# Decode attention: VectorE scores 12 of 32 columns with one multiply and one sum per chunk, values become the stationary operand, and w1 and w2 share the key and value slots

## The chip, the core and the metric

The kernel runs on one core of a Trainium2 chip. The core has engines that run side by side, each through its own instructions in order: TensorE (PE in the profile; PEld is its loading of stationary operands), VectorE (DVE), ScalarE (ACT), GpSimd (POOL) and SyncE (SP), which here only issues DMA transfers. Sixteen DMA engines move data between HBM and the on-chip memory SBUF; TensorE writes its results into PSUM. The metric is device time in microseconds (us); lower is better.

## What is computed

One token is decoded through an attention block over a key and value cache and a small dense block. Cut to what matters:

```python
# x: (1,1,640); k_cache, v_cache: (1,32,32768,192); wq: (640,6144); wo: (6144,640); all bf16
q = layernorm(x) @ wq                                   # 32 heads of 192
scores = einsum("bhqd,bhkd->bhqk", q, k_cache) * 192**-0.5
o = einsum("bhqk,bhkd->bhqd", softmax(scores), v_cache)
h = x + o.reshape(1, 1, 6144) @ wo
out = h + maximum(layernorm(h) @ w1, 0) @ w2            # w1: (640,1536), w2: (1536,640)
```

The caches hold 805 MB of the 825 MB that the core reads, and each of their elements is used once.

## The kernel before, in words

A head's 32,768 keys are cut into 8 chunks (NC) of 4,096 keys, so there are 256 chunks (G), counted by `g`. In a chunk each of the 128 partitions holds J = 32 whole rows ("columns" below) of 192 elements: 12,288 bytes a partition, 1,536 KB for the keys (`kt`, line 97) and as much for the values (`vt`, line 99). Each of the two has 5 buffers. SP issues all transfers in program order, one queue for everything, and holds back the load of a buffer until the work on its former content is done. Every transfer is spread evenly over the 16 DMA engines: of a `kt` each engine moves 8 rows of 12,288 bytes.

The program is emitted under a hand-written order (`manual_schedule`), one chunk after the other, and each engine follows it:

- `transposes(g)`: the last JP = 10 columns are turned on TensorE, 15 blocks of 128x128, into PSUM (`tp`, line 195), and ScalarE copies them in two pieces to SBUF (`kT`, line 196).
- `pv(g - 1)`: the former chunk's values are multiplied by its probabilities. The probabilities of one column are the stationary operand (128x1), the 192 values of the column the moving one; 32 matmuls add up in one PSUM row `o_ps` (line 245).
- `scores_pe(g)`: with `kT` as the stationary operand and the query (`qm`) as the moving one, 15 matmuls give the scores of the 10 columns (lines 205 to 209); ScalarE takes exp into `pB` and sums it (line 212).
- `scores_dve(g)`: VectorE scores the other 22 columns, one instruction a column that multiplies `kt` by the query spread over partitions (`qb`) and sums along the row (line 225; the profile shows a second instruction for each, DVE_READ_ACCUMULATOR). `exp_dve` takes exp of them into `pA` (line 232).

Once a head the sums of exp (`dsums`) are added over partitions by a matmul (`den_mm`, line 252), VectorE makes the reciprocal (`den_rec`, lines 258 and 259), called in the middle of the next chunk's scores, and ScalarE scales the head's row (`o_scale`, line 265). For every two heads `o_turn` (line 273) turns the row into a column with three transposes and `project` (line 283) multiplies it by `wo`. `q_rows` and `q_spread` prepare the next head's query. w1 and w2 are loaded whole into buffers of their own in the middle of the run (lines 299 and 301). After the last chunk come the last `pv`, `den_mm`, `den_rec`, `o_scale`, `o_turn`, `project`, the second layernorm (lines 130 to 145), the residual put into two PSUM rows (line 336), the first dense layer (line 341), the second one with `h1T` as the stationary operand and rows of w2 moving (lines 346 and 348), the copies to `y_row` and the store (line 353).

Of the kernel before, what the change touches and what calls it, by code (L numbers as in the profile page):

```python
# [13 lines left out]
def kernel(  # L14
# [26 lines left out]
    J = 32  # L41
    CH = P * J
    NC = Sk // CH
    G = H * NC
    JP = 10
    JD = J - JP
    NB = JP * Dh // P
    QG = 4
    assert Sk % CH == 0 and 2 * Dh == 3 * P and JP % 2 == 0 and H % QG == 0 and H % 2 == 0
# [7 lines left out]
    tsb = ctx.enter_context(tc.tile_pool(name="tsb", bufs=3))  # L57
# [36 lines left out]
    def load_kv(g):  # L94
        h, c = divmod(g, NC)
        kt = kpool.tile([P, J * Dh], bf16, name="kt")
        nc.sync.dma_start(out=kt[:], in_=k_hd[h, c * CH:(c + 1) * CH, :].rearrange("(p j) d -> p (j d)", p=P))
        vt = vpool.tile([P, J * Dh], bf16, name="vt")
        nc.sync.dma_start(out=vt[:], in_=v_hd[h, c * CH:(c + 1) * CH, :].rearrange("(p j) d -> p (j d)", p=P))
        kt_t[g], vt_t[g] = kt, vt  # L100

# [9 lines left out]
    ones_col = const.tile([P, 1], f32)  # L111
    nc.vector.memset(ones_col[:], 1.0)
# [7 lines left out]
    dsums = const.tile([P, H, 2 * NC], f32)  # L120
    w1_sb = const.tile([P, DT, Dff], bf16)
    w2_sb = const.tile([P, FT, D], bf16)
    o_pair = [const.tile([1, 2 * Dh], f32, name=f"o_pair{i}") for i in range(2)]
# [25 lines left out]
    with tc.manual_schedule():  # L149
# [37 lines left out]
        def transposes(g):  # L187
            kt = kt_t[g]
            kT = tsb.tile([P, NB, P], bf16, name="kT")
            for b0 in range(0, NB, 8):  # L190
                nb = min(8, NB - b0)
                tp = tps.tile([P, 8, P], bf16, name="tp")
                for b in range(nb):
                    off = JD * Dh + (b0 + b) * P
                    nc.tensor.transpose(out=tp[:, b, :], in_=kt[:, off:off + P], identity=ident_b[:])  # L195
# [3 lines left out]
        def scores_pe(g):  # L199
            kT = kT_t.pop(g)  # L200
            h, c = divmod(g, NC)
            qm = qm_t[h]
            sp = sps.tile([P, JP], f32, name="sp")
# [7 lines left out]
            pB = pcp.tile([P, JP], bf16, name="pB")  # L211
            nc.scalar.activation(out=pB[:], in_=sp[:], func=F.Exp, scale=SCALE,  # L212
# [3 lines left out]
        def scores_dve(g, mid=None):  # L216
            kt = kt_t.pop(g)
            h, c = divmod(g, NC)
            qb = qb_t[h]
            sc = scp.tile([P, JD], f32, name="sc")  # L220
            for j in range(JD):
                if j == 4 and mid is not None:
                    mid()
                st = scp.tile([P, Dh], bf16, name="st")
                nc.vector.scalar_tensor_tensor(out=st[:], in0=kt[:, j * Dh:(j + 1) * Dh], scalar=1.0, in1=qb[:],  # L225
                                               op0=A.mult, op1=A.mult, accum_out=sc[:, j:j + 1])
            return sc

        def exp_dve(g, sc):
            h, c = divmod(g, NC)  # L230
            pA = pcp.tile([P, JD], bf16, name="pA")
            nc.scalar.activation(out=pA[:], in_=sc[:], func=F.Exp, scale=SCALE,  # L232
# [3 lines left out]
        def pv(g):  # L236
            h, c = divmod(g, NC)
# [4 lines left out]
            for jj in range(J):  # L242
                j = jj + JD if jj < JP else jj - JP
                p = pA[:, j:j + 1] if j < JD else pB[:, j - JD:j - JD + 1]
                nc.tensor.matmul(o[:], lhsT=p, rhs=vt[:, j * Dh:(j + 1) * Dh],  # L245
                                 start=(c == 0 and jj == 0), stop=(c == NC - 1 and jj == J - 1))
# [3 lines left out]
        def den_mm(h):  # L250
            d = mm_bank([1, 2 * NC], f32, "den")
            nc.tensor.matmul(d[:], lhsT=ones_col[:], rhs=dsums[:, h, :], start=True, stop=True)  # L252
            den_t[h] = d
# [130 lines left out]
```

## Time and profile before

| | |
|---|---|
| time, median of 3 runs | 2063.01 us (2062.05 to 2064.38) |
| the profiled execution | 2062.24 us |
| its span, first to last instruction | 2060.4 us |
| granted TensorE clock, mean | 0.835 of full speed |
| busy: DVE / PE / PEld / ACT | 78% / 68% / 58% / 32% of the span |
| median from the issue of a `kt` transfer to its landing | 30.5 us |

The busy shares are means over the whole span. DMA share and GB/s by slice tell how fast the cache comes in. A row of a group gives the line, engine, operation, tiles and shapes, the count, then busy time, the mean duration of one in ns and the idle time of the engine before it. A row of the chain of waits gives start, length and what ran. In the timeline "x15" are fifteen instructions merged in one row.

### The profile page before, as it was taken

How to read it: one execution, taken by the hardware profiler on the slowest of the kernel's cores; microseconds unless marked ns; L12 is line 12 of the kernel's file. 1: busy time of each engine (PE TensorE's matmuls, PEld its weight loads, DVE VectorE, ACT ScalarE, POOL GpSimd, SP SyncE). 2: the span in 40 equal slices, each digit the busy share in tenths (PEclk: the TensorE clock that was granted, in tenths of full speed). 3: DMA queues.
4: the chain of work that ended last, by engine and by line, in shares of the span. 5: the costliest groups of instructions: out<-in, count | busy, mean ns of one | idle time of the engine just before them, and what ended most of it. 6: DMA issues, size and time to landing. Idle time of an engine off the chain costs nothing. (4 is left out here: it accounts for less than half of the span.)

```text
span 2060.4 us, 48468 instructions
## 1 busy us (share of the span) xinstructions
PE 1405.5 (68%) x16643; PEld 1193.5 (58%) x16643; DVE 1603.1 (78%) x11352; ACT 651.6 (32%) x1719; POOL 0.7 (0%) x6
## 2 busy tenths in 40 slices
PE   5766666766667666666665666766677667677767
PEld 4555555655555555555555555555566556566555
DVE  6877887778787788777777778887778877788775
ACT  3333333333333233322322333332333323333332
POOL 0000000000000000000000000000000000000000
PEclk9888887788898788888888888898788987878787
DMA  9999999999999999989998999999999989999991
GB/s 395 423 421 420 423 421 423 407 422 420 423 422 357 423 418 423 416 346 425 382 420 344 418 423 421 423 423 393 425 421 422 414 350 423 420 423 417 397 412 77
DMA packets 87844, 828.10 MB, mean 402 GB/s; under 512 B 8619, under 2 KB 21420, under 8 KB 22060
## 3 DMA queue, kind: packets, MB, share of 16 engines
q1 hardware_dynamic: 87596, 825.00, 96.5%
q8 instruction: 130, 2.13, 0.4%
q14 instruction: 118, 0.97, 0.1%
HBM read 824.97 MB, written 0.00 MB: 400 GB/s over the span
## 5 line engine op out<-in xcount | busy, mean ns | idle before, releaser
L225 DVE SCALAR_TENSOR_TENSOR st<-kt,qb 128x192 bf16<-128x192 bf16 x5632 | 1589.7, 350 | 306.7 <-DMA kt<-in_A_k_cache_dram 294.7
L195 PE MATMUL tp<-ident_b,kt 128*128 128x128 bf16 x3840 | 335.3, 255 | 596.6 <-DMA kt<-in_A_k_cache_dram 596.6
L195 PEld LDWEIGHTS <-kt 128*128 128x128 bf16 x3840 | 280.5, 116 | 623.8 <-DMA kt<-in_A_k_cache_dram 623.8
L245 PE MATMUL o_ps<-vt,pA 128*1 128x192 bf16 x5632 | 606.0, 272 | 45.8 <-ACT pA L232 45.6
L245 PEld LDWEIGHTS <-pA 128*1 128x1 bf16 x5632 | 524.9, 95 | 106.4 <-ACT pA L232 55.9
L196 ACT COPY kT<-tp 128x1024 bf16<-128x1024 bf16 (+1 forms) x512 | 465.1, 960 | 347.6 <-PE tp L195 347.3
L225 DVE DVE_READ_ACCUMULATOR st<-kt,qb 128x1 f32 x5632 | 442.4, 79 | 0.1
L245 PE MATMUL o_ps<-vt,pB 128*1 128x192 bf16 x2560 | 354.6, 305 | 0.4 <-ACT pB L212 0.4
L245 PEld LDWEIGHTS <-pB 128*1 128x1 bf16 x2560 | 237.2, 101 | 73.2 <-issue 22.8
L212 ACT ACTIVATE pB<-sp 128x10 bf16<-128x10 f32 x256 | 46.3, 181 | 630.9 <-PE sp L209 627.3
L232 ACT ACTIVATE pA<-sc 128x22 bf16<-128x22 f32 x256 | 56.6, 221 | 397.0 <-DVE st L225 396.8
L205 PEld LDWEIGHTS <-kT 128*128 128x128 bf16 x1280 | 100.0, 96 | 44.2 <-issue 43.3
L205 PE MATMUL sp<-qm,kT 128*128 128x2 bf16 x1280 | 122.3, 166 | 0.4 <-ACT kT L196 0.4
L209 PE MATMUL sp<-qm,kT 128*128 128x1 bf16 x1280 | 118.8, 163 | 0.4 <-ACT kT L196 0.4
L207 PE MATMUL sp<-qm,kT 128*128 128x1 bf16 x1280 | 118.7, 163 | 0.0
L258 DVE TENSOR_REDUCE rec<-den 1x1 f32<-1x16 f32 x32 | 5.2, 162 | 132.8 <-PE den L252 132.8
L207 PEld LDWEIGHTS <-kT 128*128 128x128 bf16 x1280 | 102.6, 96 | 0.0
L209 PEld LDWEIGHTS <-kT 128*128 128x128 bf16 x1280 | 101.4, 95 | 0.5 <-ACT kT L196 0.5
L212 ACT ACTIVATION_READ_ACCUMULATOR pB<-sp 128x1 f32 x256 | 49.9, 195 | 0.1
L232 ACT ACTIVATION_READ_ACCUMULATOR pA<-sc 128x1 f32 x256 | 48.1, 188 | 0.1
L163 PE MATMUL qps<-wq,xn_ln 128*1 128x192 bf16 x160 | 18.7, 248 | 3.3 <-DMA wq<-in_A_wq_dram 3.3
L265 ACT ACTIVATE o_pair<-o_ps,rec 1x192 f32<-1x192 f32 x32 | 13.2, 413 | 8.3 <-DVE rec L259 8.3
(62 smaller groups left out, 145.8 us busy)
## 6 DMA issues: line engine op xcount, KB each, us to landing
kt<-in_A_k_cache_dram SPq DMA_DIRECT2D x256, 1536.0 KB, 30.5
vt<-in_A_v_cache_dram SPq DMA_DIRECT2D x256, 1536.0 KB, 29.0
wq<-in_A_wq_dram SPq DMA_DIRECT2D x8, 960.0 KB, 27.1
wo<-in_A_wo_dram SPq DMA_DIRECT2D x16, 480.0 KB, 28.2
w_sb<-in_B_w_dram SPq DMA_DIRECT2D x2, 1920.0 KB, 32.2
x_row<-in_A_x_dram SPq DMA_DIRECT2D x1, 1.2 KB
out_dram<-y_row SPq DMA_DIRECT2D x1, 1.2 KB
```

What stands on the lines that cost most here:

```text
L163: nc.tensor.matmul(qps[:], lhsT=xnT[:, c:c + 1], rhs=wq[:, c, hh * Dh:(hh + 1) * Dh], start=(c == 0), stop=(c == DT - 1))
L195: nc.tensor.transpose(out=tp[:, b, :], in_=kt[:, off:off + P], identity=ident_b[:])
L196: nc.scalar.copy(out=kT[:, b0:b0 + nb, :], in_=tp[:, 0:nb, :])
L205: nc.tensor.matmul(sp[:, 2 * i:2 * i + 2], lhsT=kT[:, 3 * i + 1, :], rhs=qm[:, 1:3], start=True, stop=False, skip_group_check=True)
L207: nc.tensor.matmul(sp[:, 2 * i:2 * i + 1], lhsT=kT[:, 3 * i, :], rhs=qm[:, 0:1], start=False, stop=False, skip_group_check=True)
L209: nc.tensor.matmul(sp[:, 2 * i + 1:2 * i + 2], lhsT=kT[:, 3 * i + 2, :], rhs=qm[:, 3:4], start=False, stop=True, skip_group_check=True)
L212: nc.scalar.activation(out=pB[:], in_=sp[:], func=F.Exp, scale=SCALE, accum_out=dsums[:, h, 2 * c + 1:2 * c + 2])
L225: nc.vector.scalar_tensor_tensor(out=st[:], in0=kt[:, j * Dh:(j + 1) * Dh], scalar=1.0, in1=qb[:], op0=A.mult, op1=A.mult, accum_out=sc[:, ...
L232: nc.scalar.activation(out=pA[:], in_=sc[:], func=F.Exp, scale=SCALE, accum_out=dsums[:, h, 2 * c:2 * c + 1])
L245: nc.tensor.matmul(o[:], lhsT=p, rhs=vt[:, j * Dh:(j + 1) * Dh], start=(c == 0 and jj == 0), stop=(c == NC - 1 and jj == J - 1))
L258: nc.vector.reduce_sum(out=s[:, 0:1], in_=d[:], axis=mybir.AxisListType.X)
L265: nc.scalar.activation(out=o_pair[(h // 2) % 2][0:1, (h % 2) * Dh:(h % 2 + 1) * Dh], in_=o[:], func=F.Copy, scale=s[0:1, 1:2])
```

## The change

- The last chunk of the last head is split into three chunks of 16, 8 and 8 columns, so that there are 258 chunks. A table `chunks` gives each its head, place, columns (`jc`) and columns for TensorE (`jp`).
- TensorE takes 20 of 32 columns (10 of 16, 4 of 8): 30 transposes, four copies on ScalarE and 30 score matmuls a chunk. VectorE takes 12: one multiply of all 12 columns at once by the query (broadcast) into an f32 tile `pr`, and one sum along the rows.
- `pv` takes the values as the stationary operand, 128x128, and one or two columns of probabilities as the moving one: 48 matmuls a chunk that add up in four PSUM columns `o_ps` [128, 4]. The output is then already a column, in pieces: `o_scale` moves to VectorE and scales them by a reciprocal that is now made on all partitions (`den_mm` with a full f32 matrix of ones), and `o_turn` puts the pieces in place with 10 f32 matmuls by selection matrices (`sel`) that are made at the start.
- `den_rec` and `o_scale` are called after `scores_dve` of the next head's first chunk, not in it. At the end `den_mm` and `den_rec` stand ahead of the last `pv`.
- w1 and w2 have no buffers of their own: they are loaded in four pieces into `kt` and `vt` buffers ahead of the last three chunks. `kT` has two buffers for three.
- The second dense layer has w2 as the stationary operand and gives a column; the residual is added on VectorE, and one transpose makes the rows that are stored.

```diff
+    chunks = []
+    for h in range(H):
+        parts = [(J, 20)] * NC
+        if h == H - 1:
+            parts = [(J, 20)] * (NC - 1) + [(16, 10), (8, 4), (8, 4)]
...
-    tsb = ctx.enter_context(tc.tile_pool(name="tsb", bufs=3))
+    tsb = ctx.enter_context(tc.tile_pool(name="tsb", bufs=2))
+    prp = ctx.enter_context(tc.tile_pool(name="prp", bufs=1))
...
+    def load_w(name, src, pool, tag, c0, c1):
+        t = pool.tile([P, J * Dh], bf16, tag=tag, name=tag)
+        n = src.shape[1]
+        v = t[:, 0:(c1 - c0) * n].rearrange("p (c n) -> p c n", n=n)
+        nc.sync.dma_start(out=v, in_=src.rearrange("(c p) n -> p c n", p=P)[:, c0:c1, :])
...
-            for j in range(JD):
-                if j == 4 and mid is not None:
-                    mid()
-                st = scp.tile([P, Dh], bf16, name="st")
-                nc.vector.scalar_tensor_tensor(out=st[:], in0=kt[:, j * Dh:(j + 1) * Dh], scalar=1.0, in1=qb[:],
-                                               op0=A.mult, op1=A.mult, accum_out=sc[:, j:j + 1])
+            pr = prp.tile([P, JDM, Dh], f32, name="pr")
+            nc.vector.tensor_tensor(out=pr[:, 0:JD, :], in0=kt[:, 0:JD * Dh].rearrange("p (j d) -> p j d", d=Dh),
+                                    in1=qb[:].unsqueeze(1).to_broadcast([P, JD, Dh]), op=A.mult)
+            sc = scp.tile([P, J], f32, name="sc")
+            nc.vector.reduce_sum(out=sc[:, 0:JD], in_=pr[:, 0:JD, :], axis=mybir.AxisListType.X)
...
-                o_t[h] = ops.tile([1, Dh], f32, name="o_ps")
+                o_t[h] = ops.tile([P, 4], f32, name="o_ps")
...
-                nc.tensor.matmul(o[:], lhsT=p, rhs=vt[:, j * Dh:(j + 1) * Dh],
-                                 start=(c == 0 and jj == 0), stop=(c == NC - 1 and jj == J - 1))
+                v = vt[:, j * Dh:(j + 2) * Dh]
+                nc.tensor.matmul(o[:, 0:1], lhsT=v[:, 0:P], rhs=p[:, 0:1],
+                                 start=first, stop=False, skip_group_check=True)
+                nc.tensor.matmul(o[:, 1:3], lhsT=v[:, P:2 * P], rhs=p,
+                                 start=False, stop=False, skip_group_check=True)
+                nc.tensor.matmul(o[:, 3:4], lhsT=v[:, 2 * P:3 * P], rhs=p[:, 1:2],
+                                 start=False, stop=last, skip_group_check=True)
...
-            nc.tensor.matmul(d[:], lhsT=ones_col[:], rhs=dsums[:, h, :], start=True, stop=True)
+            nc.tensor.matmul(d[:], lhsT=ones_mat[:], rhs=dsums[:, h, :], start=True, stop=True)
...
-            nc.scalar.activation(out=o_pair[(h // 2) % 2][0:1, (h % 2) * Dh:(h % 2 + 1) * Dh], in_=o[:],
-                                 func=F.Copy, scale=s[0:1, 1:2])
+            nc.vector.tensor_scalar_mul(out=o_part[h % 4][:], in0=o_t.pop(h)[:], scalar1=s[:, 1:2])
...
-                nc.tensor.transpose(out=ps[:, b:b + 1], in_=o_pair[pr % 2][0:1, b * P:(b + 1) * P],
-                                    identity=ident_f[0:1, 0:1])
+            parts = [(0, "all", e, 0), (0, "u_l", e, 2), (0, "l_u", e, 3),
+                     (1, "l_l", e, 1), (1, "u_l", e, 3), (1, "l_u", o, 0), (1, "u_u", o, 2),
+                     (2, "all", o, 3), (2, "u_l", o, 0), (2, "l_u", o, 1)]
+            for i, (b, w, src, r) in enumerate(parts):
+                nc.tensor.matmul(ps[:, b:b + 1], lhsT=sel[w][:], rhs=src[:, r:r + 1], start=(i == 0), stop=(i == len(parts) - 1),
+                                 skip_group_check=True)
...
+            if g == G - 3:
+                half = (DT + 1) // 2
+                load_w("w1", B_w1, kpool, "kt", 0, half)
+                load_w("w1", B_w1, vpool, "vt", half, DT)
+                load_w("w2", B_w2, kpool, "kt", 0, FT // 2)
+                load_w("w2", B_w2, vpool, "vt", FT // 2, FT)
...
-        pv(G - 1)
         den_mm(H - 1)
         den_rec(H - 1)
+        pv(G - 1)
         o_scale(H - 1)
...
-            nc.tensor.matmul(y_a[:], lhsT=h1T[:, f:f + 1], rhs=w2_sb[:, f, 0:512],
-                             start=False, stop=(f == FT - 1), skip_group_check=True)
-            nc.tensor.matmul(y_b[:], lhsT=h1T[:, f:f + 1], rhs=w2_sb[:, f, 512:D],
-                             start=False, stop=(f == FT - 1), skip_group_check=True)
...
+        for n in range(DT):
+            for f in range(FT):
+                nc.tensor.matmul(yps[:, n:n + 1], lhsT=w_t["w2", f][:, n * P:(n + 1) * P], rhs=h1T[:, f:f + 1],
+                                 start=(f == 0), stop=(f == FT - 1))
```

How instructions stand in the programs is shown at three places. The first is VectorE at the first change of head; rows of the program before (`st` is the product that nobody reads, `sc` the scores, `x180` one row for equal instructions that follow each other):

```order
L145 TENSOR_SCALAR xn_ln_149<-x_col,mv,rs 128x5
L225 SCALAR_TENSOR_TENSOR st,sc<-kt,qb 128x192 x180
L258 TENSOR_REDUCE rec<-den 1x1
L259 RECIPROCAL rec<-rec 1x1
L225 SCALAR_TENSOR_TENSOR st,sc<-kt,qb 128x192 x176
```

The same place in the changed program:

```order
L257 TENSOR_TENSOR pr<-kt,qb 128x2304
L260 TENSOR_REDUCE sc<-pr 128x12
L303 TENSOR_REDUCE rec<-den 128x1
L304 RECIPROCAL rec<-rec 128x1
L309 TENSOR_SCALAR o_part_140<-o_ps,rec 128x4
L257 TENSOR_TENSOR pr<-kt,qb 128x2304
L260 TENSOR_REDUCE sc<-pr 128x12
```

Twenty-two instructions a chunk become two; the reciprocal has moved behind the whole chunk's scores and brings the scaling along, which reads `o_ps`.

The second is TensorE inside `pv`; first the program before, two columns of a chunk (a weight load and a matmul each):

```order
L245 LDWEIGHTS pB
L245 MATMUL o_ps<-vt,pB 1x192
L245 LDWEIGHTS pB
L245 MATMUL o_ps<-vt,pB 1x192
L245 LDWEIGHTS pB
```

and two columns in the changed program:

```order
L286 LDWEIGHTS vt
L286 MATMUL o_ps<-pB,vt 128x1
L288 LDWEIGHTS vt
L288 MATMUL o_ps<-pB,vt 128x2
L290 LDWEIGHTS vt
L290 MATMUL o_ps<-pB,vt 128x1
```

Two pairs of instructions for two columns have become three, with loads of 128x128 values. In all, TensorE has 33,088 instructions in the program before and 56,843 in the changed one; VectorE, which has one row per instruction there, has 646 in the changed one.

The third is SP's queue at the end; the program before, from the last two chunks on:

```order
L97 DMA kt<-in_A_k_cache_dram 128x6144
L99 DMA vt<-in_A_v_cache_dram 128x6144
L97 DMA kt<-in_A_k_cache_dram 128x6144
L99 DMA vt<-in_A_v_cache_dram 128x6144
L353 DMA out_dram<-y_row 1x640
```

and the changed one, from the last whole chunk on:

```order
L113 DMA vt<-in_A_v_cache_dram 128x6144
L123 DMA kt<-in_B_w_dram 128x3x1536
L123 DMA vt<-in_B_w_dram 128x2x1536
L123 DMA kt<-in_B_w_dram 128x6x640
L123 DMA vt<-in_B_w_dram 128x6x640
L110 DMA kt<-in_A_k_cache_dram 128x3072
L113 DMA vt<-in_A_v_cache_dram 128x3072
L110 DMA kt<-in_A_k_cache_dram 128x1536
L113 DMA vt<-in_A_v_cache_dram 128x1536
L110 DMA kt<-in_A_k_cache_dram 128x1536
L113 DMA vt<-in_A_v_cache_dram 128x1536
L399 DMA out_dram<-y_row 5x128
```

The four weight pieces have moved from the middle of the run to a place ahead of the last three, smaller chunks.

More of the change, by code (lines that the diff above doesn't have):

```diff
@@ L331 @@
         hnT = layernorm_col(h_col, "ln2")
-        y_a = ops.tile([1, 512], f32, tag="o_ps", name="y_a")
-        y_b = ops.tile([1, P], f32, tag="o_ps", name="y_b")
-        for c in range(DT):
-            y = y_a[0:1, c * P:(c + 1) * P] if c < 4 else y_b[0:1, :]
-            nc.tensor.matmul(y, lhsT=h_col[:, c:c + 1], rhs=ident_f[:], start=(c == 0 or c == 4),
-                             stop=False, skip_group_check=True)
-        h1ps = mm_bank([P, FT], f32, "h1ps")
+        h1ps = ops.tile([P, FT], f32, tag="o_ps", name="h1ps")
         for f in range(FT):
             for c in range(DT):
-                nc.tensor.matmul(h1ps[:, f:f + 1], lhsT=w1_sb[:, c, f * P:(f + 1) * P], rhs=hnT[:, c:c + 1],
+                nc.tensor.matmul(h1ps[:, f:f + 1], lhsT=w_t["w1", c][:, f * P:(f + 1) * P], rhs=hnT[:, c:c + 1],
                                  start=(c == 0), stop=(c == DT - 1))
```

122 lines of the change are left out of this document (71 added, 51 removed).

## The prediction

> **What bounds the kernel now.** I read the page's totals first, then the stream of transfers by slice and by queue.
>
> ```profile
> span 2060.4 us, 48468 instructions
> PE 1405.5 (68%) x16643; PEld 1193.5 (58%) x16643; DVE 1603.1 (78%) x11352; ACT 651.6 (32%) x1719; POOL 0.7 (0%) x6
> ...
> GB/s 395 423 421 420 423 421 423 407 422 420 423 422 357 423 418 423 416 346 425 382 420 344 418 423 421 423 423 393 425 421 422 414 350 423 420 423 417 397 412 77
> DMA packets 87844, 828.10 MB, mean 402 GB/s; under 512 B 8619, under 2 KB 21420, under 8 KB 22060
> ...
> q1 hardware_dynamic: 87596, 825.00, 96.5%
> q8 instruction: 130, 2.13, 0.4%
> q14 instruction: 118, 0.97, 0.1%
> ```
>
> No engine is full: VectorE works 1603.1 us of 256 chunks, 6.3 us a chunk where a chunk has 2060.4 / 256 = 8.05 us. The transfers look full at 96.5%. Yet the stream runs at 423 GB/s in most slices and at 340 to 400 in a few. At 423 GB/s the 825.00 MB of data take 1950 us. They take far longer, and the end of the stream shows why. The next view sums engines over stretches; its last columns are the share of the 16 DMA engines and GB/s.
>
> ```profile
> core 0: us, PE busy (x) PEld busy (x) DVE busy (x) ACT busy (x) POOL busy (x), PEclk, DMA share, GB/s
> 100.00:300.00 200.00, 137.32 (x1634) 116.93 (x1632) 157.32 (x1117) 63.16 (x167) 0.00 (x0) 0.84 1.01 421
> ...
> 2000.00:2016.00 16.00, 11.59 (x127) 9.62 (x125) 15.09 (x109) 5.87 (x14) 0.00 (x0) 0.79 1.00 423
> ...
> 2028.00:2038.00 10.00, 8.45 (x89) 6.89 (x90) 8.83 (x63) 4.23 (x8) 0.00 (x0) 0.74 0.06 26
> ```
>
> Until 2016 us all engines run. From 2028 to 2038 the share is 0.06, one in sixteen, at 26 GB/s, a sixteenth of 423: **one DMA engine is some 20 us behind the other fifteen** and finishes alone. Every transfer needs all sixteen, so chunks arrive at that engine's pace; the others run ahead until SP may issue no more, and then stop, which makes the slow slices.
>
> What holds it back? The chain of waits gives the last `kt`; its row and those of the tail behind it:
>
> ```profile
> 2005.22 30.06 DMA kt<-in_A_k_cache_dram
> ...
> 2045.35 0.29 PE oT_ps L273 x2
> ...
> 2045.88 0.53 PE attT L283 x15
> 2046.43 0.17 DVE h_col L330
> 2046.62 0.16 DVE st L130
> ...
> 2047.01 0.56 PE ln_ps L134 x2
> 2047.57 1.79 PE y_a L336 x8
> 2049.36 0.43 PE y_b L336 x2
> 2049.79 1.70 PE h1ps L341 x60
> ...
> 2051.75 0.59 PE y_a L346
> ...
> 2057.56 0.58 ACT y_row L351
> ```
>
> The last `kt` lands at 2035.3 us. The `vt` behind it moves 8 x 12,288 bytes an engine, 3.7 us at 26 GB/s: the late engine ends at 2039. It starts at about 2, so it works 2037 us for what takes 1950: 87 us lost. Now the instruction queues. Of PE's 33,286 instructions (matmuls and loads) q8 fetches 130 blocks: 16 KB or 256 instructions a block, 64 bytes each. Blocks of q14 are 0.97 MB / 118 = 8 KB, or 128 instructions; DVE's 11,352 make 88.7 of the 118. **87 us over 88.7 blocks is 0.98 us a block.** The landing records under these views agree: from 90 to 300 us the last landing of a transfer follows the one before by 3.70 us, by 4.67 where a q14 block of VectorE's rhythm (one in 23 us) lies between, and PE's blocks in q8 never delay it. So VectorE's instruction blocks all ride on one DMA engine, which sets the end.
>
> [...]
>
> **The change part by part.** *VectorE's blocks.* 646 instructions for 11,352: 5 blocks for 89. The late engine loses 5 us, not 87, and is late no more: 2039 - 87 = 1952 for an engine that carries none.
>
> *TensorE's blocks.* 56,843 instructions for 33,088: 130 x 56,843 / 33,088 = 223 blocks. One costs 0.4% x 16 x 2060.4 / 130 = 1.0 us of an engine by the q8 row. The packet records add a delay of the packet behind it: an engine that carries one lands 1.53 us late. All on one engine they would cost 130 x 1.0 us, more than the 87 that the latest one lost, so they are spread; in the landings up to 340 us they come round over eight engines in turn (20 blocks: four engines with two, four with three). What is late next is thus each of these eight: 223 / 8 x 1.53 = 42.6 us. Bounds: 14 us if they cost their bytes alone over sixteen engines, 85 over four. I take 42.6, the spread that the landings show: **the stream ends at 1952 + 42.6 = 1994.6.** ScalarE's blocks ride on another engine; its 1,719 instructions become some 2,270, 18 blocks, and remain below that.
>
> *Does the work in a chunk keep up?* A chunk may now take 1995 / 256 = 7.8 us. Durations:
>
> ```profile
> L225 DVE SCALAR_TENSOR_TENSOR st<-kt,qb 128x192 bf16<-128x192 bf16 x5632 | 1589.7, 350 | 306.7 <-DMA kt<-in_A_k_cache_dram 294.7 <-ACT pB L212 5.8 <-ACT pA L232 4.6
> L131 DVE SCALAR_TENSOR_TENSOR sq<-h_col 128x5 f32<-128x5 f32 x1 | 0.2, 156 | 0.0
> L196 ACT COPY kT<-tp 128x1024 bf16<-128x1024 bf16 x256 | 258.2, 1009 | 347.6 <-PE tp L195 347.3
> L196 ACT COPY kT<-tp 128x896 bf16<-128x896 bf16 x256 | 233.2, 911 | 0.0
> L232 ACT ACTIVATE pA<-sc 128x22 bf16<-128x22 f32 x256 | 56.6, 221 | 397.0 <-DVE st L225 396.8
> 1007.94 1.78 PE L195 MATMUL tp<-ident_b,kt 128*128 128x128 bf16 x15 [3.96 <-DMA kt<-in_A_k_cache_dram]
> 2040.61 0.18 PE L205 MATMUL sp<-qm,kT 128*128 128x2 bf16 x1
> 2040.97 0.16 PE L209 MATMUL sp<-qm,kT 128*128 128x1 bf16 x1
> ```
>
> VectorE: 192 elements take 350 ns and 5 take 156, so 1.04 ns an element and 0.15 us beside. The multiply and the sum pass 2304 elements each: 0.15 + 2.39 = 2.54 us, 5.1 together. No row shows either at this size; from below the bound is half the slope each (2.7 us, if paired 16-bit elements went through at once), from above twice (9.9 us, if f32 counted double). I take 5.1, the row's slope. ScalarE: three copies of 1.009 and one of 768 elements, 0.81 by the two copy rows, are 3.8 us; two exp of some 0.4 with their accumulator reads make 4.6. TensorE: fifteen transposes take 1.78 us at the low clock, thirty 3.6. Fifteen score matmuls of one or two columns start within 0.36 us, 26 ns apart; 48 in `pv` take 1.25 us and 30 for scores 0.8: 5.6 in all, where `pv` alone took 2.8 or more. In a row, eight transposes (0.9), the copies (3.8) and the scores (0.8) make 5.5 to 6 us from chunk to chunk. All are under 7.8, so they lie under the stream. `kt` comes free after 2.5 us of VectorE instead of 6, so SP's queue is served no later. The added waits: `den_rec` waits on VectorE for `den_mm` behind PE's scores, some 0.7 us once a head, with the next chunk's multiply behind it; `o_turn`, 10 f32 matmuls, some 4.5 us of PE for every two heads. The 1.8 us of slack a chunk hide both within three chunks; without it they would cost 16 x 5 = 80 us. Weights in `kt` and `vt` buffers: the last `vt` waits for the `pv` of the last whole chunk, which waits for the 16-column `kt`; by the bytes between, it is issued some 2 us before its turn. I cost this at nothing, 2 us at most.
>
> *The tail.* Before, 2060.4 - 2039 = 21.4 us after the stream. Now the last `kt` lands 1 us before the end E. Multiply and sum of 768 elements (0.95 each): E + 1.0. exp, E + 1.5; the sums' f32 matmul (0.56 as L134), reciprocal and scaling, E + 2.8. `o_turn`: from 0.6 us (as one matmul like L134) to 5.6 (ten times); two loads of L134 follow in some 0.5 us, so 4.5 with overlap: E + 7.3. Copy 0.25, `project` 0.55, `h_col` 0.25: E + 8.3. The layernorm took 2.3 us from L130 on: E + 10.6. No L336 ahead: the first layer 1.75, relu 0.25, the second layer likewise 60 matmuls, 1.75, where L346 and L348 took 5.8: E + 14.4. Addition, transpose and copy, 1.0; store as before, 2060.4 - 2058.1 = 2.3: **E + 17.7**.
>
> **Sum.** 1994.6 + 17.7 = 2012.3 of span. The profiled execution is 2062.24 us, 1.8 over its span, and the median of runs is 0.8 above it: 2012.3 + 1.8 + 0.8 = 2015 us.
>
> **Rivals.** *A: fetching costs no DMA engine anything that matters*; the late engine is late by itself. For it: no view prints packets by engine. Against it: 0.98 us a block. Then the stream still ends at 2039, and only the tail gains: 2039 + 17.7 + 2.6 = 2059. *B: TensorE's blocks cost their bytes alone*, over all sixteen: 1952 + 14 + 17.7 + 2.6 = 1986. For it: the q8 row's 1.0 us. *C: TensorE's blocks fall on four engines in the denser program*: 85 us, 2057. *D, slower: VectorE becomes the bound.* If both instructions take twice the slope an element, f32 being twice the bytes, a chunk takes 9.9 us: 256 x 9.9 = 2534, some 2550 us. It decides above 7.8 us a chunk, and the kernel is slower than before above 8.05. Against it: the f32 and bf16 rows above lie on one plausible line; but none is long. That the change doesn't do what it says is out: the instruction counts are those of the built program.
>
> **How the numbers follow.** Forecast 0.64, B 0.12, A 0.07, C 0.06, D 0.08, anything else slower 0.03. The forecast's own range is 1996 (`o_turn` short, blocks at 1.0 us) to 2036 (the eight engines served unevenly by a quarter, 11 us, and 10 us of PE's added work not hidden). The range for 8 in 10 takes in B and the forecast: 1982 to 2040; A, C and D are left out. About 0.2% (4 us) can be told from no change. Faster by more: forecast, B, most of A and C, 0.85. Within: 0.05. Slower: 0.10.
>
> **What would show it.** In the changed profile: q14 falls to some 40 blocks, q8 rises to 220; slices at some 415 GB/s with fewer dips; at the end half the DMA engines, not one, finish late. VectorE about 5.1 us a chunk, with idle time that `kt` ends. If q14 falls and the stream does not end earlier, A holds; if VectorE is over 90% busy, D.

## The result and the profile after

The changed kernel takes 2007.58 us (median of 4 runs, 2007.35 to 2007.7) against 2062.53 us (2061.7 to 2064.38) for the kernel before beside it: a ratio of 0.9732, 95% interval 0.9715 to 0.9749. The forecast was 2015. The profiled execution took 2007.47 us, 1.8 over its span. The page's totals, slices and queues:

```profile
span 2005.7 us, 62124 instructions
PE 1485.8 (74%) x28712; PEld 1452.7 (72%) x28712; DVE 1333.4 (66%) x646; ACT 1066.1 (53%) x2206; POOL 0.7 (0%) x6
...
GB/s 396 423 422 422 423 422 423 420 423 424 421 424 417 423 423 422 424 405 424 423 422 423 395 425 422 423 424 396 423 422 424 423 401 424 422 424 422 423 418 171
...
q8 instruction: 224, 3.67, 0.7%
q14 instruction: 36, 0.29, 0.0%
```

VectorE's blocks are gone from q14 (118 to 36), TensorE's in q8 have risen from 130 to 224. The slices that lay at 340 to 360 GB/s now lie at 395 to 405. The groups of a chunk (count, then busy us and mean ns of one, then idle time and who ended it):

```profile
L230 PE MATMUL tp<-ident_b,kt 128*128 128x128 bf16 x7677 | 857.0, 311 | 506.1 <-DMA kt<-in_A_k_cache_dram 506.1
...
L231 ACT COPY kT<-tp 128x1024 bf16<-128x1024 bf16 x766 | 726.3, 1021 | 669.4 <-PE tp L230 669.4
L257 DVE TENSOR_TENSOR pr<-kt,qb 128x2304 f32<-128x2304 bf16 x255 | 652.4, 2558 | 602.5 <-DMA kt<-in_A_k_cache_dram 602.5
L260 DVE TENSOR_REDUCE sc<-pr 128x12 f32<-128x2304 f32 x255 | 651.0, 2553 | 26.2
```

Multiply and sum take 2.56 and 2.55 us, and VectorE's idle time is ended by `kt`: the work in a chunk waits for the stream. Two stretches by engine (the last columns are the granted clock, the share of the 16 DMA engines and GB/s):

```profile
core 0: us, PE busy (x) PEld busy (x) DVE busy (x) ACT busy (x) POOL busy (x), PEclk, DMA share, GB/s
1960.00:1970.00 10.00, 7.90 (x142) 7.81 (x140) 7.68 (x4) 6.23 (x11) 0.00 (x0) 0.68 0.50 207
...
100.00:300.00 200.00, 150.93 (x2868) 147.59 (x2869) 133.26 (x61) 107.20 (x224) 0.00 (x0) 0.57 1.01 422
```

Where the program before had one DMA engine at work alone (0.06, 26 GB/s), here half of them are (0.50, 207 GB/s), until SP may issue again. The landing records show the same: at 1000 us the sixteen landings of one transfer fall into eight within 2.2 us of the last and eight some 16 to 17 us ahead. The last packet of a `vt` ends at 1988.1 us, for 2038.5 before. The end of the chain of waits (start, length, what ran):

```profile
1988.45 0.81 ACT kT L231
1990.17 0.62 PE den L297 x2
1991.08 4.41 PE oT_ps L320 x20
1995.73 0.55 PE attT L330 x15
1996.88 0.57 PE ln_ps L167 x2
1998.80 1.75 PE h1ps L384 x60
2000.80 1.75 PE yps L391 x60
2002.80 0.39 PE ytp L396
```

The tail is 2005.7 - 1988.1 = 17.6 us, 4.4 of them in `o_turn`.

The last `vt`, a piece of 8 columns, is not set by the late engines. SP issues it only when the `pv` of the last whole chunk has freed its buffer, at 1985.2 us:

```profile
1985.40 0.33 SPq L113 DMA_DIRECT2D vt<-in_A_v_cache_dram  x1
```

All sixteen engines land it within 0.5 us, at 1988.4; the `kt` before it landed at 1987.1, eight engines some 4.8 us behind the others. Pieces of this size follow each other by 0.95 to 0.99 us, so the late issue costs some 0.3 us here. In some of the runs below it costs up to 3.5, and there the landing of that last `kt` says when the late DMA engines were done.

### The profile page after: what moved, and what is told of

It reads as the page before. It is cut to its first block, busy times and chain, and to the rows that moved or that the text cites. A ratio compares the mean times of both kernels' runs of the same rounds, so it can differ in the third digit from the quotient of the medians.

```text
span 2005.7 us, 62124 instructions
## 1 busy us (share of the span) xinstructions
PE 1485.8 (74%) x28712; PEld 1452.7 (72%) x28712; DVE 1333.4 (66%) x646; ACT 1066.1 (53%) x2206; POOL 0.7 (0%) x6
## 4 chain that ended last, share of the span: by engine, by line
DMA 93%; PE 5%; DVE 1%; SPq 1%; issue 0%; ACT 0%; DVEq 0%; ACTq 0%
DMA kt<-in_A_k_cache_dram 78%; DMA vt<-in_A_v_cache_dram 15%; PE tp L230 3%; DVE pr L257 1%; PE oT_ps L320 1%; PE o_ps L288 0%; SPq L113 0%; PE o_ps L290 0%; PE o_ps L286 0%; DVE sc L260 0%; PE sp L240 0%; SPq L110 0%; PE sp L244 0%; PE sp L242 0%; PE yps L391 0%
## 5 line engine op out<-in xcount | busy, mean ns | idle before, releaser
L231 ACT COPY kT<-tp 128x1024 bf16<-128x1024 bf16 (+1 forms) x1024 | 908.0, 974 | 670.0 <-PE tp L230 670.0
L230 PE MATMUL tp<-ident_b,kt 128*128 128x128 bf16 x7677 | 857.0, 311 | 506.1 <-DMA kt<-in_A_k_cache_dram 506.1
L230 PEld LDWEIGHTS <-kt 128*128 128x128 bf16 x7677 | 794.3, 147 | 534.8 <-DMA kt<-in_A_k_cache_dram 534.8
L257 DVE TENSOR_TENSOR pr<-kt,qb 128x2304 f32<-128x2304 bf16 (+1 forms) x258 | 655.6, 2541 | 613.0 <-DMA kt<-in_A_k_cache_dram 613.0
L260 DVE TENSOR_REDUCE sc<-pr 128x12 f32<-128x2304 f32 (+1 forms) x258 | 654.3, 2536 | 26.5
L286 PEld LDWEIGHTS <-vt 128*128 128x128 bf16 x4096 | 343.4, 104 | 0.0
L288 PEld LDWEIGHTS <-vt 128*128 128x128 bf16 x4096 | 336.6, 104 | 0.0
L290 PEld LDWEIGHTS <-vt 128*128 128x128 bf16 x4096 | 326.8, 101 | 0.0
L286 PE MATMUL o_ps<-pB,vt 128*128 128x1 bf16 x2559 | 233.3, 168 | 0.0
L288 PE MATMUL o_ps<-pB,vt 128*128 128x2 bf16 x2559 | 223.8, 166 | 0.0
L290 PE MATMUL o_ps<-pB,vt 128*128 128x1 bf16 x2559 | 223.3, 164 | 0.0
L240 PEld LDWEIGHTS <-kT 128*128 128x128 bf16 x2559 | 205.1, 100 | 1.9 <-ACT kT L231 1.9
L242 PEld LDWEIGHTS <-kT 128*128 128x128 bf16 x2559 | 205.2, 100 | 0.0
L244 PEld LDWEIGHTS <-kT 128*128 128x128 bf16 x2559 | 205.1, 100 | 0.0
L286 PE MATMUL o_ps<-pA,vt 128*128 128x1 bf16 x1537 | 142.0, 164 | 0.0
L290 PE MATMUL o_ps<-pA,vt 128*128 128x1 bf16 x1537 | 142.0, 164 | 0.0
## 6 DMA issues: line engine op xcount, KB each, us to landing
vt<-in_B_w_dram SPq DMA_DIRECT2D x1, 960.0 KB, 23.8
```

Of the source, the lines that this page charges most:

```text
L231: nc.scalar.copy(out=kT[:, b0:b0 + nb, :], in_=tp[:, 0:nb, :])
L240: nc.tensor.matmul(sp[:, 2 * i:2 * i + 2], lhsT=kT[:, 3 * i + 1, :], rhs=qm[:, 1:3], start=True, stop=False, skip_group_check=True)
L242: nc.tensor.matmul(sp[:, 2 * i:2 * i + 1], lhsT=kT[:, 3 * i, :], rhs=qm[:, 0:1], start=False, stop=False, skip_group_check=True)
L244: nc.tensor.matmul(sp[:, 2 * i + 1:2 * i + 2], lhsT=kT[:, 3 * i + 2, :], rhs=qm[:, 3:4], start=False, stop=True, skip_group_check=True)
L257: nc.vector.tensor_tensor(out=pr[:, 0:JD, :], in0=kt[:, 0:JD * Dh].rearrange("p (j d) -> p j d", d=Dh), in1=qb[:].unsqueeze(1).to_broadcas ...
L260: nc.vector.reduce_sum(out=sc[:, 0:JD], in_=pr[:, 0:JD, :], axis=mybir.AxisListType.X)
```

## The experiments

**Theory.** The end of the stream is a base plus the loss of the worst DMA engine: each block of VectorE's instructions costs one fixed engine 0.98 us, each of TensorE's costs one of eight 1.53 us, and losses of different engines lie beside each other. The rivals are those of the prediction: fetching is free, or costs bytes alone, or four engines carry it. Ends of streams below are the end of the last `kt` or `vt` packet in the records; the last `kt` is given by its last landing.

**VectorE's blocks back, at the same columns.** The changed kernel with one instruction a column for its 12 columns:

```diff
-            nc.vector.tensor_tensor(out=pr[:, 0:JD, :], in0=kt[:, 0:JD * Dh].rearrange("p (j d) -> p j d", d=Dh),
-                                    in1=qb[:].unsqueeze(1).to_broadcast([P, JD, Dh]), op=A.mult)
...
-            nc.vector.reduce_sum(out=sc[:, 0:JD], in_=pr[:, 0:JD, :], axis=mybir.AxisListType.X)
+            for j in range(JD):
+                st = scp.tile([P, Dh], bf16, name="st")
+                nc.vector.scalar_tensor_tensor(out=st[:], in0=kt[:, j * Dh:(j + 1) * Dh], scalar=1.0, in1=qb[:],
+                                               op0=A.mult, op1=A.mult, accum_out=sc[:, j:j + 1])
```

> The changed kernel, but VectorE scores its 12 columns with one instruction a column as the kernel before did. Its work a chunk falls from 5.1 us to about 3.4 (12 x 0.28), its instructions rise from 646 to some 6,280 with the accumulator reads, 49 blocks of 128. Theory (instruction blocks hold back the DMA engine that carries them): that engine loses 49 x 0.98 = 48 us where the eight that carry TensorE's blocks lose some 36 (stream end 1988 against 1952), so the stream ends 12 us later: 2019 us. Rival (the gain came from a faster VectorE or from work taken off it): no slower than the changed kernel's 2007.6 us.

Measured: 2012.19 us (2012.08 to 2012.3), ratio 0.976 (0.9743 to 0.9776). Its totals:

```profile
span 2010.4 us, 67532 instructions
PE 1488.1 (74%) x28712; PEld 1454.6 (72%) x28712; DVE 904.6 (45%) x6278; ACT 1065.8 (53%) x2206; POOL 0.7 (0%) x6
...
q8 instruction: 224, 3.67, 0.7%
q14 instruction: 78, 0.64, 0.1%
```

VectorE does 429 us less work, and the kernel is 4.6 us slower. The stream ends at 1992.7, and in the landing records one engine is last again: near the end TensorE's eight land 5 to 8 us ahead of it. So blocks do delay, and they don't add: 42 more of them at 0.98 us would be 41 us, and 4.6 came. The size was below the theory's: with 49 blocks on its engine, 1992.7 puts the base at 1945, not at the prediction's 1952.

**TensorE's blocks.** 48 more score matmuls a chunk, into a column that nobody reads:

```diff
-            sp = sps.tile([P, J], f32, name="sp")
+            sp = sps.tile([P, 64], f32, name="sp")
...
+            for i in range(48):
+                nc.tensor.matmul(sp[:, 48:49], lhsT=kT[:, i % (3 * JP // 2), :], rhs=qm[:, 0:1],
+                                 start=True, stop=True, skip_group_check=True)
```

> The changed kernel with 48 more matmuls of one column a chunk, into a PSUM column that nobody reads: 24,768 TensorE instructions more, 97 blocks. Theory (blocks round over eight engines): 97 / 8 x 1.29 to 1.53 = 15.6 to 18.5 us more, 2023 to 2026 us. TensorE's own time rises by 48 x 26 ns = 1.25 us a chunk, to 6.8, still under the stream's 7.7. Rival (blocks cost nothing, TensorE has slack): 2008 us. Rival (TensorE is near its bound): more than 2030, with DMA slices far under 423 GB/s all along and TensorE's wait for kt gone.

Measured: 2029.82 us (2029.64 to 2031.67), ratio 0.9847 (0.9833 to 0.9862).

```profile
PE 1810.8 (89%) x41096; PEld 1774.0 (87%) x41096; DVE 1330.6 (66%) x646; ACT 1068.1 (53%) x2206; POOL 0.7 (0%) x6
...
q8 instruction: 321, 5.26, 1.0%
```

97 blocks more, and the stream ends at 2006.6, 18.5 us later (the last `kt` 18.3): 97 / 8 x 1.53 = 18.6. By bytes alone over sixteen engines it would have been 97 x 1.0 / 16 = 6, over four engines 37. The tail grew by 3.7 us, which is the dose in the last three chunks (3 x 48 x 26 ns). With 28 blocks an engine the changed kernel's base is 1988.1 - 42.8 = 1945 again.

The rival that TensorE is near its bound can't be put aside by the time alone. Of its signs one is there: the transposes' idle time falls from 506 us to 72.5, of which `kt` ends 26, and the chain that ended last runs over PE.

```profile
PE 71%; DMA 20%; issue 8%; ACT 0%; DVE 0%; SPq 0%; ACTq 0%; DVEq 0%
...
L230 PE MATMUL tp<-ident_b,kt 128*128 128x128 bf16 x7677 | 847.5, 307 | 72.5 <-issue 45.3
```

But the late DMA engines don't run dry: from 100 to 1900 us fewer than eight packets are under way at once for 8.5 us in all, for 10.3 in the changed kernel, and at 1000 and 1500 us eight engines land within 3 us of the last, the other eight 16 to 17.5 us ahead. So here, too, the late engines set the pace, with TensorE close behind.

**Blocks of an engine that does nothing else.** 44 one-element GpSimd memsets a chunk, as many instructions as VectorE had before, once in the changed kernel and once in the kernel before:

```diff
+    idle = const.tile([1, 8], f32, name="idle")
...
+            for i in range(44):
+                nc.gpsimd.memset(idle[0:1, i % 8:i % 8 + 1], 0.0)
             transposes(g)
```

> The changed kernel with 44 memsets of one element a chunk on GpSimd, which does nothing else and for which nobody waits: 11,352 instructions, as many as VectorE had before. Theory: 88.7 blocks x 0.98 = 87 us on one DMA engine, 51 more than the 36 of the eight: the stream ends at about 2039 as before the change and the time is 2058 us, with one DMA engine alone at the end. Rival (fetching costs the stream nothing): 2008 us. If GpSimd's blocks were spread over eight engines as TensorE's: 11 to 14 us on each, 2007 to 2021.

> The kernel before with the same 44 memsets a chunk on GpSimd. Theory (the latest DMA engine alone sets the end): if GpSimd's blocks ride on another engine than VectorE's, 87 us there lie beside VectorE's 87: no change, 2062 us. If they ride on the same engine they add: 2062 + 87 = 2149 us. Rival (fetching takes bandwidth from all sixteen): 88.7 blocks x 1 us / 16 = 5 us, 2068.

Measured: 2048.8 us (2048.45 to 2049.01), ratio 0.9937 (0.9922 to 0.9952), in the changed kernel; 2089.78 us (2086.34 to 2090.31), ratio 1.0133 (1.0118 to 1.0148), in the kernel before. Instructions of which none touches a key, a value or a score take back 41.2 of the 55 us. Stretches of the first:

```profile
core 0: us, PE busy (x) PEld busy (x) DVE busy (x) ACT busy (x) POOL busy (x), PEclk, DMA share, GB/s
...
200.00:400.00 200.00, 130.34 (x2535) 127.69 (x2533) 118.19 (x55) 93.60 (x195) 175.12 (x5204) 0.58 0.97 374
...
600.00:800.00 200.00, 151.00 (x2906) 147.73 (x2907) 137.26 (x63) 109.58 (x227) 0.00 (x0) 0.59 1.01 422
```

The dose was not spread as meant: GpSimd waits for nobody, so all its blocks come in the first 440 us, and none after; from 200 to 400 us the stream runs at 374 GB/s. At 300 us the landing records have one engine 26 us behind the other fifteen, in both runs. The others got no farther ahead than 28 us there, so the rule of the worst engine holds for stretches only. So the kernel before gives neither nothing nor the whole 87 us, and these two runs don't measure the price of a block. The tile `idle` also moved all buffers by 32 bytes; what that does is told under the buffers' address below.

**Fewer TensorE columns; the last chunk whole.** Both beside the changed kernel itself:

> The changed kernel itself, as the base of the runs beside it. Expected as measured: 2007.6 us, ratio to the kernel before 0.973.

```diff
-        parts = [(J, 20)] * NC
+        parts = [(J, 16)] * NC
```

> The changed kernel, but TensorE scores 16 columns of 32 for 20, VectorE 16 for 12. TensorE's instructions fall from 56,843 to 50,723, so some 24 blocks fewer, 3 on each of eight engines. Theory (the end of the stream is set by TensorE's blocks, 1.53 us each, over eight DMA engines): 3.0 x 1.53 = 4.6 us less, 2003 us, although VectorE works 6.7 us a chunk for 5.1. Rival (blocks cost their bytes over sixteen engines): 1.5 us less, 2006. Rival (the stream now ends by itself, blocks cost nothing): 2007.6 or more.

```diff
-            parts = [(J, 20)] * (NC - 1) + [(16, 10), (8, 4), (8, 4)]
+            parts = [(J, 20)] * NC
```

> The changed kernel with the last chunk whole, 32 columns, not split into 16, 8 and 8. Theory: the stream ends as before it; behind the last landing VectorE's multiply and sum take 2.54 each for 0.95 (8 columns) and pv 48 matmuls for 12, but kt is there 3.7 us earlier against vt, so the tail grows by 1 to 1.5 us: 2008.6 to 2009.1. Rival (the split is a main part of the gain): 2015 or more. Rival (pieces of 8 columns cost the stream more than they save): under 2007.

Measured: the changed kernel 2007.19 us (2006.84 to 2007.93), ratio 0.9734 (0.9721 to 0.9748); 16 columns 2003.23 (2002.88 to 2003.44), ratio 0.9714 (0.9701 to 0.9728); whole chunk 2008.42 (2008.01 to 2008.67), ratio 0.974 (0.9726 to 0.9753). Giving VectorE a third more columns makes the kernel 4.0 us faster; TensorE has 24 blocks fewer, three on each of eight engines. The last packet ends 2.6 to 3.0 us earlier (1985.1, for 1988.1 and 1987.7 in the changed kernel's two profiles), but the late issue of the last `vt` costs some 2 us here. The last `kt` lands at 1982.4, for 1987.1 and 1986.4: 4.0 to 4.7 us earlier, where the theory has 3 x 1.53 = 4.6. The split of the last chunk is worth 1.2 us.

**Fewer instructions everywhere, and a miss.** Two columns of probabilities are stationary and 384 values move, into two rows of which the crossing halves are unused; TensorE scores 14 columns, VectorE 6 with one instruction each and 12 with two:

```diff
+                o_t[h] = ops.tile([2, 2 * Dh], f32, tag="o_ps", name="o_ps")
...
-                nc.tensor.matmul(o[:, 0:1], lhsT=v[:, 0:P], rhs=p[:, 0:1],
-                                 start=first, stop=False, skip_group_check=True)
...
+                nc.tensor.matmul(o[:], lhsT=p, rhs=vt[:, j * Dh:(j + 2) * Dh],
+                                 start=(c == 0 and i == 0), stop=(c == NCH[h] - 1 and i == len(order) - 1))
...
+            nc.scalar.activation(out=t[:, n:n + Dh], in_=o[:, 0:Dh], func=F.Copy, scale=s[0:2, 1:2])
+            nc.scalar.activation(out=t[:, 2 * Dh + n:3 * Dh + n], in_=o[:, Dh:2 * Dh], func=F.Copy, scale=s[0:2, 1:2])
...
+                for r in range(2):
+                    nc.tensor.matmul(ps[:, b:b + 1], lhsT=t[:, 2 * Dh * r + b * P:2 * Dh * r + (b + 1) * P],
+                                     rhs=ident_f[0:2, r:r + 1], start=(r == 0), stop=(r == 1))
```

> The changed kernel with fewer instructions everywhere: probabilities are stationary again, but two columns at a time (128x2) with 384 moving values, into two PSUM rows whose crossing halves are unused; TensorE scores 14 columns; VectorE 6 columns by one instruction each and 12 by multiply and sum. TensorE's instructions fall from 56,843 to 31,135 (122 blocks, 15.3 on each of eight engines), VectorE's rise to some 3,700 (29 blocks on one). Theory (stream ends at 1945 + the loss of the worst engine): 1945 + max(15.3 x 1.53 = 23.4, 29 x 0.97 = 28) = 1973, with a tail of some 16 to 17 us a span of 1990 and a time of 1992 us. Rival (the stream of 825 MB can end no earlier than about 1988 whatever the blocks): 2006 or more. Rival (TensorE's moving columns become the bound at a low clock, over 7.7 us a chunk): 2010 or more.

Measured: 1971.28 us (1970.81 to 1971.77), ratio 0.956 (0.9547 to 0.9573), 20 us below the theory. The lines that show why are the slices and the group of the new matmul:

```profile
span 1969.9 us, 38918 instructions
...
GB/s 399 428 427 428 428 427 429 427 427 429 427 428 425 429 428 427 428 427 427 428 428 429 421 428 428 429 428 422 429 427 428 428 407 428 428 429 428 428 428 181
...
q8 instruction: 123, 2.02, 0.4%
q14 instruction: 57, 0.47, 0.1%
...
L286 PE MATMUL o_ps<-vt,pA 128*2 128x384 bf16 x2302 | 456.1, 347 | 0.0
```

Undisturbed slices run at 428 GB/s, not at 423: the base itself is faster. The packet records say how: nearly every packet of 12,288 bytes takes 460 ns here, while before and in the changed kernel most records lie between 460 and 473. The built programs say what else differs. `kt` and `vt` buffers begin at a multiple of 256 bytes in this kernel, 128 bytes past one in the changed kernel, 32 past one in the kernel before: tiles that the change adds to and takes from the constants shift all that comes behind them.

**The buffers' address alone.** An unused tile ahead of all others, in the changed kernel and (480 bytes) in the kernel before:

```diff
     const = ctx.enter_context(tc.tile_pool(name="const", bufs=1))
+    pad = const.tile([P, 64], bf16, name="pad")
```

> The changed kernel and nothing else but an unused tile of 128 bytes a partition in the constants, so that the kt and vt buffers (and wq, wo) begin at multiples of 256 bytes in SBUF; in the changed kernel they begin 128 bytes past one, in the kernel before 32, in the run with pairs of columns at one. Theory (the start address of a buffer sets how long a DMA packet of 12,288 bytes takes: mean of the records under 480 ns 464.8 ns before, 463.5 changed, 460.0 in the run with pairs): packets of 460.0 ns, and some 1930 us of them 0.76% shorter: 14.6 us less, 1992.5 us. Rival (the packets of the run with pairs are short because its engines run fewer instructions or read SBUF in other strides): 2007 us, packets as in the changed kernel.

> The kernel before with an unused tile of 480 bytes a partition, so that its kt and vt buffers begin at multiples of 512 bytes, not 32 bytes past one. Theory (start address): packets of 460.0 ns for 464.8, 1.03% of some 1950 us: 20 us less, 2042 us, and the late engine's 87 us for VectorE's blocks stay. Then the change is worth 2042 - 1992.5 = 49.5 us between aligned kernels, and some 5 to 6 us of its 55 came from the buffers' new address. Rival: 2062 us, unchanged.

Measured: the changed kernel 1987.43 us (1986.99 to 1988.22), ratio 0.9639 (0.9626 to 0.9652), 19.8 us below its time without the tile; the kernel before 2031.21 us (2029.83 to 2032.27), ratio 0.985 (0.9837 to 0.9864), 30.7 us faster than without. Stretches of the kernel before with the tile:

```profile
core 0: us, PE busy (x) PEld busy (x) DVE busy (x) ACT busy (x) POOL busy (x), PEclk, DMA share, GB/s
100.00:300.00 200.00, 136.42 (x1657) 116.51 (x1658) 160.07 (x1137) 64.99 (x173) 0.00 (x0) 0.85 1.01 427
...
1998.00:2008.00 10.00, 6.93 (x84) 6.17 (x85) 8.91 (x63) 4.03 (x8) 0.00 (x0) 0.83 0.06 26
```

and of the changed kernel with the tile:

```profile
100.00:300.00 200.00, 154.56 (x2936) 150.59 (x2934) 134.72 (x63) 109.03 (x230) 0.00 (x0) 0.59 1.01 427
```

From 100 to 300 us both run at 427 GB/s, for 421 and 422 without the tile. The one late engine is still there in the kernel before with the tile (0.06, 26 GB/s, the same as without it). Both gains are larger than expected (14.6 and 20 us). The expectation went by the packets' own length; the landing records hold the gaps between packets, too: a quiet step in this table is the time from one transfer's last landing to the next one's where no block comes between (3.4 to 4.2 us, from 90 to 1900 us):

| kernel | `kt` begins past a multiple of 256 bytes | mean packet (records under 480 ns) | quiet step, median | last `vt` packet ends |
|---|---|---|---|---|
| before | 32 | 464.8 ns | 3.697 us | 2038.5 us |
| before, with the tile | 0 | 460.1 | 3.638 | 2008.5 |
| changed | 128 | 463.5 | 3.689 | 1988.1 |
| changed, with the tile | 0 | 460.0 | 3.644 | 1968.1 |
| pairs of columns | 0 | 460.0 | 3.647 | 1955.0 |

512 transfers with a step shorter by 0.059 us are 30 us (measured 30.0), by 0.045 us 23 (measured 20.0). The tile `idle` put the buffers of the two runs with GpSimd's dose 160 and 64 bytes past a multiple of 256, with packets of 463.1 ns in both and quiet steps of 3.689 and 3.690 us: no change for the changed kernel, and some 4 us less for the kernel before.

Why a packet of 12,288 bytes took 464.8 or 463.5 ns at those two addresses and 460.0 at the aligned one, and which part of the chip takes the extra time, no run here shows.

**Values no longer stationary.** The changed kernel with `pv`, `o_scale` and `o_turn` as before the change; its tiles happen to put the buffers at a multiple of 256 bytes, so it stands against 1987.43:

```diff
+                nc.tensor.matmul(o[:], lhsT=p, rhs=vt[:, j * Dh:(j + 1) * Dh],
+                                 start=(c == 0 and i == 0), stop=(c == NCH[h] - 1 and i == len(order) - 1))
```

> The changed kernel with the values no longer stationary: probabilities 128x1 as the stationary operand, 192 values moving, the row scaled on ScalarE and turned by three transposes, as before the change; buffers begin at multiples of 512 bytes. TensorE's instructions fall from 56,843 to 48,507, 4.1 blocks fewer on each of eight engines. Theory: against the changed kernel with aligned buffers 6.2 us less of stream, and 4 us less of tail (three transposes for the 4.3 us of ten f32 matmuls): 1982 us. Rival (values as the stationary operand are a part of the gain): 1992.5 or more. Rival (192 moving columns a matmul and thirty transposes are more than TensorE does in 7.6 us): 2000 or more, TensorE over 90% busy.

Measured: 1980.08 us (1979.84 to 1980.58), ratio 0.9603 (0.959 to 0.9616). This part of the change costs 7.4 us. By the last packet 4.0 of them lie in the stream (1964.1 for 1968.1) and 3.6 in the tail (14.0 for 17.6). But the last `vt` comes 3 us late here, since the `pv` that frees its buffer now takes 3.75 us at the end, for 1.3 in the changed kernel. By the last `kt` the late engines are done 6.3 us earlier (1960.6 for 1966.9), as expected (6.2), and what follows it is 1.2 us shorter (17.5 for 18.7), where 4 were expected. TensorE is no bound, by the totals and by its transposes' idle time, which `kt` ends:

```profile
PE 1595.9 (81%) x24344; PEld 1445.7 (73%) x24344; DVE 1325.5 (67%) x614; ACT 1076.5 (54%) x2238; POOL 0.7 (0%) x6
...
q8 instruction: 190, 3.11, 0.6%
```

```profile
L230 PE MATMUL tp<-ident_b,kt 128*128 128x128 bf16 x7677 | 592.5, 240 | 369.1 <-DMA kt<-in_A_k_cache_dram 320.1 <-ACT kT L231 47.5
```

**The fastest version.** The run with pairs of columns, with two columns moved on VectorE from single instructions to the two long ones:

```diff
-            JS = 6 if JD > 12 else 0
+            JS = 4 if JD > 12 else 0
```

> The run with pairs of columns, but VectorE takes 4 columns by one instruction each for 6, and 14 by multiply and sum. VectorE's instructions fall from some 3,700 to 2,670, from 29 blocks to 21, so its DMA engine (last there, 4 us behind eight others) comes level with the eight that carry TensorE's 122 blocks. Theory (the worst engine alone sets the end): 4 us less, 1967 us. Rival (losses of different engines add): 8 x 0.97 = 8 us less, 1963. Rival (VectorE, at 7.1 us of 7.6 a chunk, is the bound): 1971 or more, idle time of VectorE near nothing.

Measured: 1968.02 us (1967.28 to 1968.6), ratio 0.9544 (0.9531 to 0.9557).

```profile
span 1966.8 us, 37898 instructions
...
PE 1486.8 (76%) x15802; PEld 950.8 (48%) x15802; DVE 1811.4 (92%) x2654; ACT 843.3 (43%) x2015; POOL 0.7 (0%) x6
...
q14 instruction: 49, 0.40, 0.0%
```

VectorE works 61 us more, at 92% of the span, and the kernel is 3.3 us faster: eight blocks left the engine that was last, which came level with TensorE's eight, and the last `kt` lands 3.4 us earlier (1948.0 for 1951.5). That is nearer to the 4 us of the worst engine than to the 8 of a sum. This version is 4.6% faster than the kernel before and 2% faster than the changed one.

## Why the prediction was right, and where it was off

The forecast's mechanism is what the runs show, and its time was 7.4 us above the measured one. Its gain of 48 us stands beside 55 measured, made of two parts: between the two kernels with aligned buffers the change is worth 2031.21 - 1987.43 = 43.8 us, and the other 11 are the difference of the 30.7 and 19.8 us that the two addresses cost, of which the prediction knew nothing.

- *One late engine, by VectorE's blocks.* Right. With 49 blocks back an engine falls behind again; with half the engines late the share is 0.50 for 0.06. At 0.98 us a block 88.7 blocks are 87 us, and steps with a block are 4.62 us for 3.64 in the aligned kernel before.
- *"1952 for an engine that carries none".* This is the term that was mis-sized. It was right for the old address: 2038.5 - 87 = 1951.5. But the change moved the buffers from 32 to 128 bytes past a multiple of 256, and there the base is 1945. So 1994.6 became 1988.1. With aligned buffers it is 1921 in the kernel before (2008.5 - 87) and 1925 in the changed one (1968.1 - 42.8). The address thus took some 10 us off the base, and some 4 came back by something that no run shows; that the forecast of the stream missed by 6.5 us and not by 10 is luck.
- *TensorE's blocks over eight engines, 42.6 us.* Right in number (224 blocks for 223) and place; the added dose gave 18.5 us for 18.6, and blocks taken away gave as much: the last `kt` lands 4.0 to 4.7 us earlier with 16 columns, 6.3 with values moving (4.2 blocks, 6.5). The table behind this list puts the runs side by side.
- *Work hidden in the chunk.* Right: 2.56 and 2.55 us for 2.54 each, 1.02 for a copy of 1.009, and idle time that `kt` ends. The clock granted to TensorE fell from 0.835 to 0.60, which the prediction had not expected and which cost nothing that shows, since `kt` ends all of the 506.1 us of idle time before TensorE's transposes.
- *The last `vt` issued before its turn, "at nothing, 2 us at most".* The chain it named is the one that holds it back. It costs some 0.3 us in the changed kernel, and 2 to 3.5 in four of the later runs.
- *The tail, 17.7 us.* 17.6, with `o_turn` at 4.4 for 4.5.
- *The rivals.* Fetching that costs nothing (A) falls with VectorE's 4.6 us and TensorE's 18.5 us. VectorE's own waits show no such cost: `kt` ends all of the 602.5 us of idle time before its multiplies. The landings of the DMA engines show it, by the 0.98 and 1.53 us a block. Bytes alone (B) give 6 us for the 18.5, four engines (C) 37. VectorE as the bound (D) falls with its two rows. The end of the stream, 1988, lay between the forecast's 1994.6 and B's 1966, so the result alone could not part them; the dose did.

The loss of the latest engines by the prediction's 0.98 and 1.53 us a block, taken from the landing of the last `kt`, leaves the base in every run (some 1 us lower than by the last packet):

| run | blocks on each of the latest engines | loss | last `kt` lands | base |
|---|---|---|---|---|
| changed kernel | 28.0 of TensorE | 42.8 us | 1987.1 us | 1944.2 |
| one instruction a column | 49.0 of VectorE | 48.1 | 1991.7 | 1943.7 |
| 48 more score matmuls | 40.1 of TensorE | 61.4 | 2005.3 | 1943.9 |
| 16 columns | 25.0 of TensorE | 38.3 | 1982.4 | 1944.2 |
| changed, with the tile | 28.0 of TensorE | 42.8 | 1966.9 | 1924.1 |
| values moving | 23.8 of TensorE | 36.3 | 1960.6 | 1924.3 |
| pairs of columns | 28.7 of VectorE | 28.1 | 1951.5 | 1923.3 |
| the fastest version | 15.4 of TensorE | 23.5 | 1948.0 | 1924.5 |

Eight programs, with losses from 23 to 61 us and on one engine or eight, have two bases, one for each address, and agree on each within 1.2 us.

What the one number hides is that the parts of the change pull against each other. The gain comes from VectorE's fewer instructions; the shorter tail gives some 4 us (21.9 to 17.6), 1.2 of them by the split of the last chunk (its other parts were not run one by one); values as the stationary operand take 7.4 us away.

## What to carry to other kernels

Where a stream of DMAs sets the time, as here, count instructions, not work: here a block of 128 VectorE instructions went with 0.98 us of delay on one DMA engine, a block of 256 TensorE instructions with 1.53 us on one of eight, and the latest of the sixteen engines set the end. Losses on different engines lay beside each other: 42 more blocks on one engine, 41 us of its time, cost 4.6 us here beside the 42.8 us that eight others lose. Look at landings of one transfer over its engines before looking at any busy share. And when a change shifts what lies in SBUF ahead of large DMA buffers, print where these begin: an unused tile was worth 20 and 31 us here, and the difference between 32 and 128 bytes past some 11 by these two runs, though no run moved one kernel from the one to the other.

## What was not expected of the hardware

The start address of a DMA's target in SBUF: buffers at a multiple of 256 bytes gave packets of 460.0 ns and 427 GB/s, buffers 32 or 128 bytes past one 464.8 and 463.5 ns and 421 to 422 GB/s, at 12,288 bytes a packet. The address is not all: with 48 more matmuls a chunk and the same 128 bytes the packets took 462.7 ns. 256 and 512 bytes were not told apart as the multiple: the changed kernel's tile gave 256 past a multiple of 512, the others 0, and both gave 460 ns. Why the packets took longer at 32 bytes past (464.8 ns) than at 128 (463.5 ns), in two different kernels, stays open; the records don't name the engine of a packet.

In these runs the granted TensorE clock went with the form of the matmuls, not with TensorE's busy share: 0.61 with values as the stationary operand at 75% busy, 0.922 with probabilities stationary at 81%, both with aligned buffers; 48 more score matmuls a chunk made TensorE 89% busy and left the clock at 0.614. Why is open. The same transposes take 311 ns in the changed kernel and 240 with probabilities stationary.
